# Row sums of the first batch as products with ones, fewer fillers, and conversions set back, in a fused attention and two-layer MLP kernel

## The chip, the cores and the metric

The kernel runs on one core of one Trainium2 chip. The metric is the device time of one execution in microseconds. The time before the change is 966.98 us, the median of three runs (966.38 to 970.47).

## The reference

Decayed causal attention feeds two token-wise layers. With S = 576, D = 64, four batches and eight heads:

```python
scores = q @ k.T / 8 + cum[:, None] - cum[None, :]      # cum: running sum of log f
scores = where(causal, -1e9, scores); scores -= scores.max(-1)
attn = exp(scores); attn = attn / (attn.sum(-1) + 1e-9)
x = (attn @ v) as [2304, 512]
h = max(x @ w1, x @ w2, x @ w3)            # 512 -> 768
x = h @ w_out                              # 768 -> 512
h = x @ w_in                               # 512 -> 2048
P = a0 + a1*h + a2*h**2 + a3*h**3;  Q = 1 + |b0|*|h| + |b1|*h**2
out = (P / (Q + 1e-6)) @ w_out2            # 2048 -> 512
```

The weights of the layers come as 64-bit floats, and the kernel gets their bits.

## The kernel before

**Attention.** The 32 heads go in pairs. A pair's 576 queries fall into group 0 (queries 0 to 320, in blocks 0 to 2) and group 1 (320 to 576, blocks 3 and 4). A `Unit` is one head of a pair and one group; the units in order are the slots. The first batch has eight pairs: pairs 0 to 3 do group 0 alone, two slots each, and pairs 4 to 7 group 1 alone. Later pairs do both groups, four slots. There are 64 slots, 16 of them of the first batch.

In the loop over slots (L539 to L582) three units are in flight. The newest does its `scores`: for each block, score products on TensorE into a bank with tag `s` (L343, or the split form L345 and L346), on VectorE the mask and the minimum of the negated scores in one operation (L347), on ACT the exponential, whose accumulator gives the row sums (L353). Then `normalise` adds 1e-9 to the sums and inverts them on VectorE (L358, L359), one column per block, and POOL multiplies each block by its inverse (L362). One slot later `turn` transposes the blocks on TensorE into banks with tag `t` (L382), and ACT copies them into `pt`, keys on partitions (L384). Two slots later `attend`, for the second head of the pair, does the value products of both heads into one bank with tag `o` (L398), the two heads on different columns of the array, and ACT and VectorE write the result as a high part and a low part, `x` (L405, L406).

**Fillers.** `exercised` (L80) issues `WARM` products of a constant with itself into each new bank of pairs 0 to 3 ahead of its proper use. Nothing reads them. A pair has 13 such banks: two of transposed q and k, six of scores, four of turned blocks and one of values.

**First layer.** `moe1_units` makes 18 units `moe1_h` (L423, twelve products each, a running maximum in tag `mx` with three buffers) and four units `moe1_o` (L446) per batch and group. `fill` (L504), called six times per slot, hands them out.

**Conversions.** A weight tile is loaded as raw 64-bit words by SP (L160) and turned into a high and a low single-precision part by `convert` (L162 to L179): ACT takes the magnitude, VectorE runs four operations, ACT copies the high part, POOL subtracts. `conv` has 30 of them, 18 of 128x512 for w1 to w3 and twelve of 128x256 for the first layer's output weights. Loads are traced two units ahead. The raw tiles of the 18 rotate through six buffers of tag `x2`, so that a load waits until the last VectorE operation has read the tile that held its buffer. `conv_due` sets the rate: in slots 0 to 6 each of the six calls adds 0.15 of a conversion, later 0.5.

**Order.** Each engine runs its instructions in the order of its queue. A planner that simulates the time line forms these queues: of what could run, the instruction traced earlier goes first, and `tc.high_priority` moves a block's place in that ranking. `keep_in_program_order` (`pinned`) keeps an instruction behind the one traced before it on its engine; raw loads and the copies of the decay rows (L304) on SP are pinned so. The last part of the second layer alone has an order written by hand (L766).

Of the kernel before, what the change touches and what calls it, by code (L numbers as in the profile page):

```python
# [8 lines left out]
F32 = mybir.dt.float32  # L9
# [28 lines left out]
def kernel(  # L38
# [14 lines left out]
    def r32(ap):  # L53
        return ap.bitcast(F32)
# [29 lines left out]
                nc.tensor.matmul(bank, warm[:, 0], wide, start=True, stop=True)  # L84
        return bank

    WARM = 2
    mask = const.tile([P, S], F32, name="mask")
    nc.gpsimd.memset(mask, 0.0)
    nc.gpsimd.affine_select(  # L90
# [1 line left out]
        fill=-1.0e9, base=0, channel_multiplier=1,  # L92
    )


    NR = B * H
    fl = apool.tile([NR, S], F32, name="fl", tag="vs", bufs=3)
# [15 lines left out]


    LOOK, WHOLE, PRE = 2, 6, 2
    CONV2, EARLY = (32, 0.25), 12
    kqs = {}

# [40 lines left out]
        raws[nm_] = rp.tile(shape[:-1] + [2 * shape[-1]], I32, name=f"raw_{nm_}", tag=rt, bufs=rb)  # L159
        tc.keep_in_program_order(nc.sync.dma_start(raws[nm_], src.bitcast(I32)))  # L160

    def convert(hi, lo, src, nm_, pool, tag, bufs):  # L162
        shape = list(src.shape)
        raw = raws.pop(nm_)
        raw = raw.rearrange("p c (f t) -> p c f t", t=2)
        low, top = raw[:, :, :, 0], raw[:, :, :, 1]
        t = pool.tile(shape, I32, name=f"cv_{nm_}", tag=tag, bufs=bufs)
        tf = t.bitcast(F32)
        nc.scalar.activation(tf, top.bitcast(F32), AF.Abs)
        nc.vector.tensor_scalar(tf, tf, E_LO, E_HI, op0=ALU.max, op1=ALU.min)  # L170
        nc.vector.tensor_scalar(t, t, 0x07FFFFFF, 3, op0=ALU.bitwise_and, op1=ALU.logical_shift_left)
        nc.vector.scalar_tensor_tensor(
            out=t, in0=low, scalar=29, in1=t, op0=ALU.logical_shift_right, op1=ALU.bitwise_or
        )
        nc.vector.scalar_tensor_tensor(
            out=t, in0=top, scalar=-0x40000000, in1=t, op0=ALU.bitwise_and, op1=ALU.bitwise_or
        )
        nc.scalar.activation(hi, tf, AF.Copy)
        nc.gpsimd.tensor_tensor(lo, tf, r32(hi), op=ALU.subtract)  # L179

    def rows(w):
        return w.rearrange("(c p) f -> p c f", p=P)
# [1 line left out]
    def raw_w1(fc, j):  # L184
        return rows((w1, w2, w3)[j])[:, :, fc * P : (fc + 1) * P], f"w{j}_{fc}"

    def convert_w1(fc, j):
        if fc not in w1t:
            w1t[fc] = [wpool.tile([P, 3, NDC, P], F32R, name=f"w1{x}_{fc}", tag="w", bufs=12) for x in "hl"]
        hi, lo = (t[:, j] for t in w1t[fc])  # L190
        convert(hi, lo, *raw_w1(fc, j), mpool, "x0", 6)

    def raw_wo(fc, z):
        return rows(w_out)[:, fc : fc + 1, z * 256 : (z + 1) * 256], f"wo_{fc}_{z}"
# [1 line left out]
    def convert_wo(fc, z):  # L196
        if fc not in wot:
            wot[fc] = wpool.tile([P, 2, DM], F32R, name=f"wo_{fc}", tag="x2", bufs=6)
        hi, lo = (wot[fc][:, x : x + 1, z * 256 : (z + 1) * 256] for x in range(2))
        convert(hi, lo, *raw_wo(fc, z), mpool, "x0", 6)  # L200

    wpd = dram.tile([P, NF2, 2, DM], F32R, name="wpd")

# [37 lines left out]
    class Pair:  # L241


        def __init__(self, n, b, hp, groups):
            self.n, self.b, self.hp, self.groups = n, b, hp, groups
            self.ng = groups[-1] + 1
            self.nk = GBLK[groups[-1]][-1] + 1
            self.ik = [(2 * n + h) % NKB for h in range(2)]
            self.iq = [[(2 * n + h) % m for h in range(2)] for m in NQB]
            self.pt = {}  # L250
            self.whole = n < WHOLE
            self.iqf = [(2 * n + h) % 4 for h in range(2)]

        def load(self):
# [58 lines left out]
    class Unit:  # L313
# [5 lines left out]

        def begin(self):  # L320
            self.st = apool.tile([P, 9], F32, name=f"st_{self.nm}", tag="st", bufs=3)
            self.rs = apool.tile([P, 2, 3], F32, name=f"rs_{self.nm}", tag="rs", bufs=3)

        def scores(self, i):
            p, h, g = self.pair, self.h, self.g
            if not p.whole:
                (k1, k2), (q1, q2) = k_split(p.ik[h]), q_split(g, p.iq[g][h])
            nr = P
            qs = slice(Q0[i] - GQ[g][0], Q0[i] - GQ[g][0] + P)
            keys = Q1[i]  # L330
            self.e[i] = apool.tile([P, keys], F32, name=f"e{i}_{self.nm}", tag=f"e{i}_{h}")
            e = self.e[i]
            st = self.st
            n0 = 3 * (i - GBLK[self.g][0])
            nm = st[:nr, n0 : n0 + 2]
            l = self.rs[:nr, 0, i - GBLK[self.g][0] : i - GBLK[self.g][0] + 1]
            parts = [(0, keys)] if keys <= 512 else [(0, 320), (320, keys)]
            off = S - P - Q0[i]
            for n, (a, z) in enumerate(parts):
                sp = exercised(ps_s.tile([P, 512], F32, name=f"s{i}_{n}_{self.nm}", tag="s"), p.n)  # L340
                if p.whole:
                    kf, qf = kfs[p.ik[h]][: D + 2], qfs[p.iqf[h]][: D + 2]
                    nc.tensor.matmul(sp[:nr, : z - a], qf[:, qs], kf[:, a:z], start=True, stop=True)  # L343
                else:
                    nc.tensor.matmul(sp[:nr, : z - a], q1[:, qs], k1[:, a:z], start=True, stop=False)  # L345
                    nc.tensor.matmul(sp[:nr, : z - a], q2[:, qs], k2[:, a:z], start=False, stop=True)  # L346
                nc.vector.tensor_tensor_reduce(  # L347
                    out=e[:nr, a:z], in0=sp[:nr, : z - a], in1=mask[:nr, off + a : off + z],
                    scale=-1.0, scalar=3.0e38 if n == 0 else nm[:, 0:1],
                    op0=ALU.add, op1=ALU.min, accum_out=nm[:, n : n + 1],  # L350
                )
            m = nm[:, len(parts) - 1 : len(parts)]
            nc.scalar.activation(e[:nr], e[:nr], AF.Exp, bias=m, scale=-1.0, accum_out=l)  # L353

        def normalise(self):
            blks = GBLK[self.g]
            n = len(blks)
            nc.vector.tensor_scalar_add(self.rs[:, 0, :n], self.rs[:, 0, :n], 1.0e-9)  # L358
            nc.vector.reciprocal(self.rs[:, 1, :n], self.rs[:, 0, :n])  # L359
            for j, i in enumerate(blks):  # L360
                e = self.e[i]
                nc.gpsimd.tensor_scalar(e, e, self.rs[:, 1, j : j + 1], 0.0, op0=ALU.mult, op1=ALU.add)  # L362
# [23 lines left out]
        def attend(self):  # L386
# [6 lines left out]
            ot = exercised(ps_o.tile([P, 512], F32, name=f"o_{self.nm}", tag="o"), p.n)  # L393
            order = list(GCH[g].items())
            with tc.high_priority():
                for j, (c, (col, q0)) in enumerate(order):
                    for i in (1, 0):
                        mm = nc.tensor.matmul(  # L398
                            ot[SIDES[i][0], q0 - lo : w], p.v[:, c, i], p.pt[g][:, i, col : col + hi - q0],
                            start=(j == 0), stop=(j == len(order) - 1),  # L400
                        )
                        if (j, i) != (0, 1):
                            pinned(mm)
            x = mpool.tile([P, 2, w], F32R, name=f"x_{self.nm}", tag=f"x{g}", bufs=(6, 8)[g])
            nc.scalar.activation(x[:, 0], ot[:, :w], AF.Copy)  # L405
            nc.vector.tensor_tensor(x[:, 1], ot[:, :w], r32(x[:, 0]), op=ALU.subtract)  # L406
            xt[p.b, p.hp, g] = x


    hs = {}  # L410
# [113 lines left out]
    state["c"] = state["c2"] = 0.0  # L524

    def conv_due(step):
        state["c"] += 0.15 if step < 7 else 0.5
        return NCONV - int(state["c"])

    pairs[0].load()  # L530
# [267 lines left out]
```

## Time and profile before

| what | value |
|---|---|
| median of three runs | 966.98 us |
| profiled execution | 970.9 us |
| its span, first to last instruction | 969.1 us |
| mean granted clock of TensorE | 0.988 |
| TensorE busy (PE) | 943.1 us, 97% |
| VectorE busy (DVE) | 739.6 us, 76% |
| ScalarE busy (ACT) | 623.8 us, 64% |
| GpSimd busy (POOL) | 252.4 us, 26% |

PE is TensorE's matmuls and PEld its weight loads, DVE is VectorE, ACT ScalarE, POOL GpSimd, SP the engine that issues the transfers. A line such as L362 is line 362 of the kernel below. A record of TensorE is one pass, and an fp32 matmul leaves two records, so a count of twelve in L398 is six matmuls. [...] Busy times of TensorE are modelled, since matmuls are pipelined. The shares over the whole span average stages with different limits, so the rows further down go by stage: the stretch, its length, the busy time and in brackets the instructions of each engine that took part, the granted clock, the share of the 16 DMA engines and GB/s.

### The profile page before, as it was taken

Reading aid. Unit: us, or ns where it says so; the run is one execution under the profiler, and the core shown is the slowest. Engines: PE = TensorE matmul, PEld = TensorE weight load, DVE = VectorE, ACT = ScalarE, POOL = GpSimd, SP = SyncE. Lnnn points to the kernel's source line nnn. Section 1 sums busy time; section 2 is a strip of 40 time slices with the busy share of each in tenths; the row PEclk is TensorE's granted clock in tenths of the full one; section 3 lists DMA queues with packets and bytes.
Section 4 is the critical chain, followed back from the end, with each engine's and each line's share of the span. In section 5 each row is a group of like instructions: output and inputs, shape, how many; then the busy total and the mean of one; then the engine's idle time right before and its main releaser. Section 6 shows DMA issues by size and latency. Waiting matters only on the chain.

```text
span 969.1 us, 16846 instructions
## 1 busy us (share of the span) xinstructions
PE 943.1 (97%) x5780; PEld 829.9 (86%) x5780; DVE 739.6 (76%) x1756; ACT 623.8 (64%) x1457; POOL 252.4 (26%) x408
## 2 busy tenths in 40 slices
PE   7998999999999999999999999999999999999998
PEld 6767889998998988999999978888888888999997
DVE  5789985557777777534397949988888988899997
ACT  5875666667667666646454548767666766677775
POOL 2646553445454545425133400000000000000000
PEclk9978999999999999999999999999999999999999
DMA  6685233124446445230145477011002101100000
GB/s 160 159 236 153 64 83 89 43 63 119 140 131 205 133 136 174 58 94 1 57 140 185 132 253 269 1 44 43 1 1 66 44 1 46 64 1 1 34 1 33
DMA packets 125621, 88.52 MB, mean 91 GB/s; under 512 B 74448, under 2 KB 110304, under 8 KB 125536
## 3 DMA queue, kind: packets, MB, share of 16 engines
q1 hardware_dynamic: 125536, 87.45, 30.4%
q8 instruction: 46, 0.75, 0.4%
q14 instruction: 39, 0.32, 0.1%
HBM read 64.73 MB, written 22.69 MB: 90 GB/s over the span
## 4 chain that ended last, share of the span: by engine, by line
PE 70%; DVE 14%; DMA 6%; ACT 4%; issue 3%; POOL 2%; SPq 1%; ACTq 0%; POOLq 0%; DVEq 0%
PE oo L721 7%; PE oo L722 7%; PE oo L720 7%; PE hq L671 6%; PE hq L673 6%; PE hq L672 6%; PE tp L382 4%; PE h L430 4%; PE o L398 4%; PE h L431 4%; PE h L432 4%; PE x2p L455 2%; DMA raw_wi<-in_moe_w_in_dram 2%; PE x2p L456 2%; PE x2p L457 2%
## 5 line engine op out<-in xcount | busy, mean ns | idle before, releaser
L430 PE MATMUL h<-x,w1h 128*128 128x320 f32 (+1 forms) x576 | 176.6, 307 | 3.1 <-ACT m L435 2.2
L431 PE MATMUL h<-x,w1h 128*128 128x320 f32 (+1 forms) x576 | 172.1, 299 | 0.0
L432 PE MATMUL h<-x,w1l 128*128 128x320 f32 (+1 forms) x576 | 171.2, 298 | 0.0
L430 PEld LDWEIGHTS h<-x,w1h 128*128 128x128 f32 x576 | 109.4, 190 | 7.0 <-ACT m L435 3.0
L362 POOL TENSOR_SCALAR e<-e,rs 128x64 f32<-128x64 f32 (+4 forms) x160 | 87.7, 563 | 106.4 <-DVE rs L359 91.5
L353 ACT ACTIVATE e<-e,st 128x64 f32<-128x64 f32 (+4 forms) x160 | 89.1, 557 | 37.8 <-DVE st L347 36.0
L721 PE MATMUL oo<-wp,gh 128*128 128x512 f32 x288 | 112.9, 392 | 0.0
L720 PE MATMUL oo<-wp,gh 128*128 128x512 f32 x288 | 112.5, 390 | 0.0
L431 PEld LDWEIGHTS h<-x,w1h 128*128 128x128 f32 x576 | 109.5, 190 | 0.4 <-issue 0.2
L432 PEld LDWEIGHTS h<-x,w1l 128*128 128x128 f32 x576 | 109.2, 190 | 0.0
L722 PE MATMUL oo<-wp,gl 128*128 128x512 f32 x288 | 108.8, 392 | 0.0
L680 ACT ACTIVATE s<-hq 128x512 f32<-128x512 f32 (+1 forms) x80 | 44.3, 554 | 97.4 <-PE hq L673 97.4
L347 DVE CUSTOM_DVE_ANT_0 e<-s,mask 128x320 f32<-128x320 f32 (+3 forms) x160 | 67.2, 433 | 37.9 <-PE s L346 24.0
L384 ACT ACTIVATE pt<-tp 128x384 f32<-128x384 f32 (+3 forms) x160 | 69.8, 469 | 19.2 <-PE tp L382 17.4
L683 DVE SCALAR_TENSOR_TENSOR s<-s,ab,u 128x512 f32<-128x512 f32 (+1 forms) x80 | 55.7, 697 | 32.1 <-ACT u L681 31.9
L382 PE MATMUL tp<-ident,e 128*128 128x128 f32 (+1 forms) x480 | 78.0, 280 | 1.3 <-DVE k2s L275 0.6
L673 PE MATMUL hq<-x,wil 128*128 128x512 f32 (+1 forms) x192 | 70.4, 367 | 0.0
L671 PE MATMUL hq<-x,wih 128*128 128x512 f32 (+1 forms) x192 | 70.4, 367 | 0.0
L672 PE MATMUL hq<-x,wih 128*128 128x512 f32 (+1 forms) x192 | 70.3, 366 | 0.0
L722 PEld LDWEIGHTS oo<-wp,gl 128*128 128x128 f32 x288 | 54.1, 188 | 11.7
L720 PEld LDWEIGHTS oo<-wp,gh 128*128 128x128 f32 x288 | 54.2, 188 | 11.0
L721 PEld LDWEIGHTS oo<-wp,gh 128*128 128x128 f32 x288 | 54.1, 188 | 10.9
(129 smaller groups left out, 2433.6 us busy)
## 6 DMA issues: line engine op xcount, KB each, us to landing
raw_w<-in_moe_w_dram SPq DMA_DIRECT2D x18, 512.0 KB
raw_wp<-in_moe_w_out_dram SPq DMA_DIRECT2D x32, 256.0 KB
wpd<-wp SPq DMA_DIRECT2D x32, 256.0 KB
raw_wi<-in_moe_w_in_dram SPq DMA_DIRECT2D x32, 256.0 KB
wp<-wpd SPq DMA_DIRECT2D x10, 768.0 KB
x2d<-xo SPq DMA_DIRECT2D x16, 320.0 KB
out_dram<-ob SPq DMA_DIRECT2D x18, 256.0 KB
kn<-in_k_dram SPq DMA_DIRECT2D x32, 128.0 KB
```

What stands on the lines that cost most here:

```text
L353: nc.scalar.activation(e[:nr], e[:nr], AF.Exp, bias=m, scale=-1.0, accum_out=l)
L362: nc.gpsimd.tensor_scalar(e, e, self.rs[:, 1, j : j + 1], 0.0, op0=ALU.mult, op1=ALU.add)
L382: nc.tensor.transpose(tp[:kr, dst : dst + P], self.e[i][:, Q0[c] : Q1[c]], ident)
L430: nc.tensor.matmul(hp_[:, :w], wh[:, j, dc], xs[dc][:, 1], start=(dc == NDC - 1), stop=False)
L431: nc.tensor.matmul(hp_[:, :w], wh[:, j, dc], xs[dc][:, 0], start=False, stop=False)
L432: nc.tensor.matmul(hp_[:, :w], wl[:, j, dc], xs[dc][:, 0], start=False, stop=(dc == 0))
L671: nc.tensor.matmul(hp_[:, :w], wih[:, dc, fs], xh, start=(dc == 0), stop=False)
L672: nc.tensor.matmul(hp_[:, :w], wih[:, dc, fs], xl, start=False, stop=False)
L673: nc.tensor.matmul(hp_[:, :w], wil[:, dc, fs], xh, start=False, stop=(dc == NDC - 1))
L720: nc.tensor.matmul(o, g[0][:, ts_], wh_, start=(fc == 0), stop=False)
L721: nc.tensor.matmul(o, g[0][:, ts_], wl_, start=False, stop=False)
L722: nc.tensor.matmul(o, g[1][:, ts_], wh_, start=False, stop=(fc == NF2 - 1))
```

## The change

Four edits go together. For the first batch's eight pairs (`late`) the row sums no longer come from the exponential's accumulator, and the blocks aren't normalised ahead of the transposes. In their place `attend` first issues, into a bank with tag `t`, the same products as the value products with a 128x64 tile of ones in place of the values: that gives each query's sum on 64 partitions for each head. ACT adds 1e-9 while it reads that bank, VectorE inverts the 128x320 or 128x256 result and multiplies the values by it, and the split into high and low part reads the product from SBUF. `WARM` goes from 2 to 1. `convert` gets a `behind` offset, and the 30 first conversions are traced at a priority 400 lower. The early rate goes from 0.15 to 0.3.

```diff
-    WARM = 2
+    WARM = 1
+    tiny = const.tile([P, 1], F32, name="tiny")
+    nc.vector.memset(tiny, 1.0e-9)
+    summing = const.tile([P, D], F32, name="summing")
+    nc.vector.memset(summing, 1.0)
+    LATE = 2 * NPAIR
-    def convert(hi, lo, src, nm_, pool, tag, bufs):
+    def convert(hi, lo, src, nm_, pool, tag, bufs, behind=0):
+        with tc.high_priority(offset=behind):
...
-        convert(hi, lo, *raw_w1(fc, j), mpool, "x0", 6)
+        convert(hi, lo, *raw_w1(fc, j), mpool, "x0", 6, -400)
-        convert(hi, lo, *raw_wo(fc, z), mpool, "x0", 6)
+        convert(hi, lo, *raw_wo(fc, z), mpool, "x0", 6, -400)
+            self.late = n < LATE
-            l = self.rs[:nr, 0, i - GBLK[self.g][0] : i - GBLK[self.g][0] + 1]
+            l = None if p.late else self.rs[:nr, 0, i - GBLK[self.g][0] : i - GBLK[self.g][0] + 1]
         def normalise(self):
+            if self.pair.late:
+                return
...
-                for j, (c, (col, q0)) in enumerate(order):
-                    for i in (1, 0):
-                        mm = nc.tensor.matmul(
-                            ot[SIDES[i][0], q0 - lo : w], p.v[:, c, i], p.pt[g][:, i, col : col + hi - q0],
-                            start=(j == 0), stop=(j == len(order) - 1),
-                        )
-                        if (j, i) != (0, 1):
-                            pinned(mm)
+                if p.late:
+                    sm = ps_t.tile([P, 512], F32, name=f"sm_{self.nm}", tag="t")
+                    dsts = [(sm, lambda c, i: summing), (ot, lambda c, i: p.v[:, c, i])]
+                else:
+                    dsts = [(ot, lambda c, i: p.v[:, c, i])]
+                for n, (dst, lhs) in enumerate(dsts):
+                    for j, (c, (col, q0)) in enumerate(order):
+                        for i in (1, 0):
+                            mm = nc.tensor.matmul(
+                                dst[SIDES[i][0], q0 - lo : w], lhs(c, i), p.pt[g][:, i, col : col + hi - q0],
+                                start=(j == 0), stop=(j == len(order) - 1),
+                            )
+                            if (n, j, i) != (0, 0, 1):
+                                pinned(mm)
...
-            nc.scalar.activation(x[:, 0], ot[:, :w], AF.Copy)
-            nc.vector.tensor_tensor(x[:, 1], ot[:, :w], r32(x[:, 0]), op=ALU.subtract)
+            xn = ot
+            if p.late:
+                xn = mpool.tile([P, 320], F32, name=f"xn_{self.nm}", tag="mx", bufs=3)
+                nc.scalar.activation(xn[:, :w], sm[:, :w], AF.Identity, bias=tiny)
+                nc.vector.reciprocal(xn[:, :w], xn[:, :w])
+                nc.vector.tensor_tensor(xn[:, :w], ot[:, :w], xn[:, :w], op=ALU.mult)
+            nc.scalar.activation(x[:, 0], xn[:, :w], AF.Copy)
+            nc.vector.tensor_tensor(x[:, 1], xn[:, :w], r32(x[:, 0]), op=ALU.subtract)
...
-        state["c"] += 0.15 if step < 7 else 0.5
+        state["c"] += 0.3 if step < 7 else 0.5
```

## Rows read from the trace of the kernel before

**Rows 1.** Stages: length, busy PE, PEld, DVE, ACT, POOL (count), clock, DMA, GB/s.

```profile
11.00:52.00 41.00, 40.05 (x231) 31.25 (x232) 25.02 (x91) 31.59 (x94) 19.02 (x29) 1.00 0.65 171
52.00:62.50 10.50, 9.28 (x50) 5.87 (x48) 10.38 (x29) 9.37 (x24) 2.65 (x5) 1.00 1.14 313
62.50:79.60 17.10, 15.61 (x53) 10.03 (x54) 15.81 (x35) 10.43 (x25) 11.68 (x11) 0.50 0.58 160
79.60:137.00 57.40, 52.53 (x365) 47.88 (x364) 53.73 (x126) 35.85 (x89) 33.47 (x41) 1.00 0.35 99
137.00:148.00 11.00, 8.84 (x41) 8.04 (x41) 6.67 (x19) 5.83 (x17) 6.99 (x13) 0.69 0.44 120
148.00:490.00 342.00, 338.13 (x2665) 313.18 (x2664) 208.60 (x714) 216.11 (x623) 150.77 (x271) 1.00 0.36 103
```

**Rows 2.** Chain of waits by line, 11 to 56 us, then 56 to 142.

```profile
by line: PE s L84 12.5%; DMA raw_w<-in_moe_w_dram 11.7%; PE s L343 11.0%; PE tp L84 8.7%; POOL e L362 8.3%; issue 7.3%; PE o L398 6.0%; DMA kn<-in_k_dram 5.8%; PE tp L382 4.9%; POOL w1l L179 3.4%; PE tk L297 2.9%; DVE e L347 2.3%; DVE cv_w 
...
by line: issue 8.6%; DVE cv_w L175 6.4%; DVE cv_wo L175 6.0%; DVE e L347 6.0%; PE s L343 5.6%; DVE cv_w L172 5.3%; DVE cv_wo L172 4.5%; DVE m L437 4.4%; DVE cv_wo L170 4.3%; DMA raw_w<-in_moe_w_dram 4.3%; DMA raw_wo<-in_moe_w_out_dram 4.2%;
```

**Rows 3.** Line 84 alone, two windows: busy PE, PEld (count).

```profile
4.80:11.00 6.20, 5.28 (x14) 3.03 (x14) 1.00 0.54 121
11.00:56.00 45.00, 31.18 (x90) 14.78 (x90) 1.00 0.68 185
```

**Rows 4.** Pieces of the chain from 0 to 170 us: start, us, what.

```profile
12.64 0.47 PE s L84 x2
...
36.73 1.34 PE o L398 x12
...
152.85 2.10 PE o L398 x20
```

**Rows 5.** Timeline of TensorE: start, us, instruction, idle before.

```profile
61.20 1.02 PE L343 MATMUL s<-kf,qf 66*128 66x448 f32 x2 [0.94 <-ACT qf L283]
62.53 0.90 PE L382 MATMUL tp<-ident,e 128*128 128x128 f32 x3 [0.30 <-POOL e L362]
```

**Rows 6.** ACT by form, 0 to 150 us: count, busy, mean ns, idle.

```profile
L353 ACT ACTIVATION_READ_ACCUMULATOR e<-e,st 128x1 f32 x42 | 8.0, 189 | 0.0
...
L405 ACT ACTIVATE x<-o 128x320 fp32r<-128x320 f32 x4 | 1.7, 436 | 0.9 <-PE o L398 0.9
```

**Rows 7.** VectorE by form, 148 to 490 us.

```profile
L406 DVE TENSOR_TENSOR x<-o,x 128x320 fp32r<-128x320 f32 x12 | 5.9, 491 | 2.2 <-ACT x L405 1.8
L406 DVE TENSOR_TENSOR x<-o,x 128x256 fp32r<-128x256 f32 x13 | 5.5, 420 | 16.7 <-ACT x L405 16.7
...
L359 DVE RECIPROCAL rs<-rs 128x3 f32<-128x3 f32 x24 | 4.2, 175 | 0.6
L359 DVE RECIPROCAL rs<-rs 128x2 f32<-128x2 f32 x24 | 3.9, 164 | 0.5
```

**Rows 8.** Line 359, two windows: least/median/greatest ns, starts, forms.

```profile
L359 DVE RECIPROCAL rs<-rs x8: 169/176/177, 15.2 to 51.0; 128x3 f32<-128x3 f32 x8
...
L359 DVE RECIPROCAL rs<-rs x8: 152/154/167, 61.5 to 137.3; 128x2 f32<-128x2 f32 x8
```

**Rows 9.** Tile rs by window: busy DVE, POOL.

```profile
11.00:52.00 41.00, 3.77 (x16) 11.18 (x23) 1.00 0.65 171
52.00:137.00 85.00, 4.13 (x15) 11.76 (x16) 0.90 0.49 138
```

**Rows 10.** Tile cv_w by window: busy DVE, ACT, POOL.

```profile
11.00:52.00 41.00, 13.45 (x24) 7.89 (x13) 7.97 (x6) 1.00 0.65 171
52.00:137.00 85.00, 33.26 (x48) 14.80 (x24) 17.32 (x12) 0.90 0.49 138
```

**Rows 11.** Tile cv_wo, 52 to 137 us: busy DVE, ACT, POOL.

```profile
52.00:137.00 85.00, 21.14 (x46) 8.55 (x21) 6.70 (x9) 0.90 0.49 138
```

**Rows 12.** Timeline of SP, from 65 us.

```profile
65.70 12.20 SPq L160 DMA_DIRECT2D raw_w<-in_moe_w_dram  x3
...
79.02 0.38 SPq L232 DMA_DIRECT2D v<-in_v_dram  x1
```

More of the change, by code (lines that the diff above doesn't have):

```diff
@@ L168, in convert @@
         tf = t.bitcast(F32)
[L169 to L173, printed above, removed]
-        )
[L175 to L179, printed above, removed]
+        with tc.high_priority(offset=behind):
+            nc.scalar.activation(tf, top.bitcast(F32), AF.Abs)
+            nc.vector.tensor_scalar(tf, tf, E_LO, E_HI, op0=ALU.max, op1=ALU.min)
+            nc.vector.tensor_scalar(t, t, 0x07FFFFFF, 3, op0=ALU.bitwise_and, op1=ALU.logical_shift_left)
+            nc.vector.scalar_tensor_tensor(
+                out=t, in0=low, scalar=29, in1=t, op0=ALU.logical_shift_right, op1=ALU.bitwise_or
+            )
+            nc.vector.scalar_tensor_tensor(
+                out=t, in0=top, scalar=-0x40000000, in1=t, op0=ALU.bitwise_and, op1=ALU.bitwise_or
+            )
+            nc.scalar.activation(hi, tf, AF.Copy)
+            nc.gpsimd.tensor_tensor(lo, tf, r32(hi), op=ALU.subtract)
     def rows(w):
@@ L321, in begin @@
             self.st = apool.tile([P, 9], F32, name=f"st_{self.nm}", tag="st", bufs=3)
-            self.rs = apool.tile([P, 2, 3], F32, name=f"rs_{self.nm}", tag="rs", bufs=3)
+            if not self.pair.late:
+                self.rs = apool.tile([P, 2, 3], F32, name=f"rs_{self.nm}", tag="rs", bufs=3)
         def scores(self, i):
@@ L395, in attend @@
             with tc.high_priority():
-                for j, (c, (col, q0)) in enumerate(order):
-                    for i in (1, 0):
-                        mm = nc.tensor.matmul(
-                            ot[SIDES[i][0], q0 - lo : w], p.v[:, c, i], p.pt[g][:, i, col : col + hi - q0],
-                            start=(j == 0), stop=(j == len(order) - 1),
-                        )
-                        if (j, i) != (0, 1):
-                            pinned(mm)
+                if p.late:
[9 more added lines that the diff above has]
+                                start=(j == 0), stop=(j == len(order) - 1),
+                            )
+                            if (n, j, i) != (0, 0, 1):
+                                pinned(mm)
             x = mpool.tile([P, 2, w], F32R, name=f"x_{self.nm}", tag=f"x{g}", bufs=(6, 8)[g])
-            nc.scalar.activation(x[:, 0], ot[:, :w], AF.Copy)
-            nc.vector.tensor_tensor(x[:, 1], ot[:, :w], r32(x[:, 0]), op=ALU.subtract)
             xt[p.b, p.hp, g] = x
+            xn = ot
[6 more added lines that the diff above has]
+            nc.vector.tensor_tensor(x[:, 1], xn[:, :w], r32(x[:, 0]), op=ALU.subtract)
     hs = {}
```

## The prediction

> **What bounds the kernel now.** I read the busy time by stage first. The reader is to see four regimes [rows 1]. From 148 us on TensorE is busy without pause (338.13 of 342.00 us until 490) at the full clock, and VectorE has room (208.60 of 342.00). From 11 to 52 us TensorE is busy too (40.05 of 41.00), but VectorE is not (25.02). [...] So whatever TensorE loses ahead of 148 us is not made up later, and whatever work it is spared there comes off the end. All edits fall into this part: the first batch's eight pairs and the first 30 conversions.
>
> Second, the chain of waits for the same two parts [rows 2]. From 11 to 56 us it runs through the filler matmuls of line 84 (12.5, 8.7 and 2.9 per cent in the visible shares), raw weight loads, scores and the POOL normalisation (8.3 per cent). From 56 to 142 us the conversions' VectorE lines lead it. Third, the groups of the single instructions, for prices.
>
> **Fillers (A, 11 to 56 us).** 14 and 90 of them run by 56 us [rows 3], two at each of 52 banks; 52 go. A pair takes 0.47 us of the chain [rows 4], so 0.235 us each, 12.2 us in all. The three visible shares are 24.1 per cent of 45 us, 10.8 us, and half of it goes: -5.4 us. Bounds: 0 (something else binds at once) and -12.2.
>
> **Sums with ones, first four attends.** Each repeats the value products' shape: twelve instruction records, 1.34 us [rows 4], 5.4 us in four. That is TensorE work in the stretch that TensorE sets, so I charge it by the same share as the fillers (10.8 of the 21.2 us that 90 of them cost, one half): +2.7. Bounds 0 and 5.4.
>
> **Normalisation.** In A it is 8.3 per cent of 45 us of the chain, 3.7 us. What is late next are the raw loads (11.7 per cent) and the exponentials, so half: -1.9. Bounds 0 and -3.7. In B (52 to 148 us) the recorded wait of TensorE for it in [rows 5] is 0.30 us: -0.3. On ACT 40 reads of the accumulator at 189 ns go (7.6 us) and eight evictions of a bank come (0.436 us for 320 columns, at most 3.5 us) [rows 6]; ACT is busy 31.59 of 41.00 us [rows 1], so that is cover and I count nothing.
>
> **Reciprocals and products on VectorE.** They go from a 128x3 or 128x2 tile per unit to a 128x320 or 128x256 tile per attend. No row has that size. The product is like the subtraction of line 406, 0.491 and 0.420 us [rows 7]. For the reciprocal, 175 ns for three elements and 164 for two are 11 ns an element, so 0.175 + 317 x 0.011 = 3.66 us and 0.164 + 254 x 0.011 = 2.96 us. The low end is the subtraction's row itself (0.49 and 0.42); the high end comes from the medians in the early windows, 176 and 154 ns [rows 8], 22 ns an element, 7.15 and 5.74 us. I take the middle, the row with the most instructions of this very operation, and keep both ends.
> [...]
>
> In A the four attends bring 4 x (3.66 + 0.49) = 16.6 us; VectorE has 41.00 - 25.02 = 16.0 us idle plus the 3.77 us of row-sum operations that go [rows 9]. They fit, and 3.2 us are left. In B they bring 4 x (2.96 + 0.42) = 13.5 us, with 4.13 us going [rows 9]: +9.4 us on the engine that sets the pace. Behind each such reciprocal VectorE's queue holds the next block's score reduction, for which ACT's exponential and a score bank of TensorE wait.
>
> **Conversions.** One of w1-w3 takes VectorE 13.45/6 = 2.24 us in A and 33.26/12 = 2.77 us in B [rows 10]; beside it ACT runs two instructions, POOL one, and SP a 512 KB load. Twice the early rate hands out 12 by slot 7 instead of 6, but VectorE's 3.2 us left in A hold one more: -2.8 us in B. Lower priority lets the attention's instructions pass. The twelve wo conversions cost 21.14 us before 137 us [rows 11], and only the output products of the first layer need them; behind 148 us VectorE has 133 us of room [rows 1]. Between none and all can slip; at 21.14/11.5 = 1.84 us each I take five of twelve: -9.2 (bounds 0 and -21). POOL loses 11.76 us of normalisation in 52 to 137 us [rows 9], of 47.80 us that it is busy [rows 1]; the conversions there are 0.53 us dearer than in A, 6.4 us for twelve, and if that is contention with POOL a quarter goes: -1.6 (bounds 0 and -6.4).
>
> **Sums, last four attends.** 2.10 us each at the full clock [rows 4], 8.4 us. TensorE's 9.7 us of idle time in B [rows 1] are the cover; where the pauses lie elsewhere it is not one. A quarter shows: +2.1 (bounds 0 and 8.4; at the half clock twice that). The sums also hold one of the three banks through which the transposes rotate, and the reciprocal's tile one of the three buffers of the first layer's running maximum, for 0.4 + 3.0 + 3 x 0.4 = 4.6 us by the prices above. A maximum that waits for it keeps one of the first layer's two banks, and the products behind it on TensorE stand: 0 to 4 x 4.6 us. I take 0, since two other buffers go round.
>
> **Sum.** A: -5.4 + 2.7 - 1.9 = -4.6. B: -0.3 + 9.4 - 2.8 - 9.2 - 1.6 + 2.1 = -2.4. Together -7.0 us. The profiled execution took 970.9 us (span 969.1 and 1.8 around it), so 963.9 by its own count; it lies 3.9 us above the median of 966.98, which is what the prediction is of: 960.0 us.
>
> **Rivals.** (1) The reciprocal is dear: the mechanism on the slower side. At 22 ns an element B gets 4 x (5.74 - 2.96) = 11.1 us more, on the engine that is already full there; in A 30.6 us meet 19.8, half of the excess counts (5.4), and no conversion moves (2.8). That is +19.3: 979.3 us. For it: VectorE's full rows from 52 to 137 us. Against: the larger groups say 11 ns. It decides from some 15 ns an element on, where 4 x 254 x 4 ns = 4.1 us more in B and the 2.8 have eaten the gain of 7.0.
> (2) The clock falls in A as well. Before it fell at 62.5 us TensorE had paused 0.94 us and 0.30 us [rows 5], with the fillers over since 56 us; with half the fillers such pauses can come earlier. A half-clock stretch of 17.10 us costs 8.6 us where TensorE is the bound: 968.6 us. Against: the sums' products fill part of the place.
> [...]
> (3) Only TensorE's work counts: -12.2 + 13.8 = +1.6, so 968.6 us. For it: after 148 us nothing else binds. Against: the idle and half-clock time ahead of it, which is to be had.
> (4) The loads get in the way, and the early rate does not do what it says. SP stood 12.20 us at raw loads from 65.70 us, with a v load behind it at 79.02 [rows 12]: six buffers, each free only when its conversion has read it. With 12 handed out early and the conversions behind, this comes earlier, and the copies of the decay rows are pinned behind it. Then A's 4.6 us are lost: 964.6 us.
> (5) More than I count: with the attention first in VectorE's queue TensorE no longer pauses at 60 us and keeps the full clock: -8.6 more, 951.4 us. For it: the pauses are short, 1.24 us. Against: the wide reciprocals stand in that very place.
>
> **How the numbers follow.** No change is what lies within 0.5 per cent, about what a measurement of this kernel can tell: 962.1 to 971.8 us. Forecast 0.36, with a range of its own of 955 to 966 (0.25 faster, 0.11 same); (5) 0.20, faster; (3) 0.14 and (4) 0.08, same; (2) 0.09, 0.05 same and 0.04 slower; (1) 0.13, slower. Faster 0.45, same 0.38, slower 0.17. If all pauses (10.7 us from 11 to 148 us), the half clock's 8.6 + 3.4 us and the fillers went and only the sums' 13.8 us came, it would be 946 us; the low end of 949 is just above. The high end of 976 takes in (2) twice and most of (1).
>
> **What would show it.** Right: 52 fillers; the attend of a pair twice as long; no POOL normalisation ahead of batch two; line 406's neighbour, a wide reciprocal, at 2.3 to 3.7 us; TensorE without pause from an earlier time than 148 us, by about as much as the gain; wo conversions behind that time. Wrong: a wide reciprocal of 5 us or more, or of 0.5; a granted clock of 0.5 ahead of 56 us; SP standing at raw loads ahead of 56 us with score products late behind it; VectorE full but no later than now, with the same pauses of TensorE.

## The result and the profile after

The changed kernel takes 978.28 us (median of four runs, 976.40 to 982.21) against 967.64 for the kernel before on the same chip (the 966.98 of the prediction with a fourth run). The ratio is 1.0104 with a 95% interval of 1.0085 to 1.0122: about 10 us slower, where 7 us faster was forecast. The profiled execution took 976.4 us, its span is 974.6 (before 970.9 and 969.1): it was the fastest of its four, and that of the kernel before took 3.3 us more than its median, so the two traces lie 5.5 us apart and not 10.

The stages, in the windows and columns of [rows 1]:

```profile
11.00:52.00 41.00, 37.07 (x227) 27.39 (x227) 36.99 (x93) 33.18 (x77) 10.16 (x8) 0.96 0.90 244
52.00:62.50 10.50, 8.34 (x49) 4.61 (x47) 10.50 (x21) 9.58 (x22) 4.96 (x4) 1.00 0.79 216
62.50:79.60 17.10, 13.98 (x59) 7.88 (x59) 17.00 (x35) 11.23 (x21) 5.47 (x4) 0.70 0.59 185
79.60:137.00 57.40, 48.72 (x347) 41.78 (x344) 47.99 (x115) 33.98 (x81) 22.79 (x32) 0.97 0.22 56
137.00:148.00 11.00, 10.11 (x67) 7.57 (x68) 6.34 (x26) 6.70 (x24) 5.60 (x14) 0.84 0.27 62
148.00:490.00 342.00, 340.40 (x2674) 318.19 (x2671) 203.31 (x692) 215.35 (x609) 148.07 (x266) 1.00 0.36 101
```

From 11 to 52 us VectorE has become nearly full (36.99 of 41.00 us, before 25.02), and TensorE idles 3.93 us there (before 0.95). Over the five stretches ahead of 148 us TensorE idles 18.8 us; before it was 10.7. The half clock (0.50 in the clock records, where 1.00 is full speed) does not explain that difference: in these stretches its records add up to 20.5 us, before to 23.9. From 148 us on TensorE is as full as it was.

The chain of waits by line, 11 to 56 us and 56 to 142 us, as in [rows 2]:

```profile
by line: DVE cv_w L179 15.8%; DVE xn L427 13.9%; DVE cv_w L182 11.1%; DVE e L356 10.9%; issue 10.1%; DVE cv_w L177 9.4%; DVE cv_w L178 9.2%; PE s L352 6.4%; DVE x L430 3.7%; DMA kf<-ncd 3.3%; PE s L84 3.1%; DVE xn L428 1.8%; PE tp L393 1.7%
...
by line: DVE e L356 8.6%; issue 7.3%; DVE xn L427 6.3%; DVE cv_w L182 5.9%; DVE cv_w L179 5.6%; DVE cv_wo L177 4.7%; DVE cv_w L177 4.6%; PE tp L393 4.4%; DVE cv_w L178 4.3%; DVE cv_wo L179 4.2%; DVE cv_wo L178 2.9%; DMA raw_wo<-in_moe_w_out
```

The fillers (L84) have left the head of the first chain. In their place stand four VectorE lines of conversions (cv_w, 45.5% together) and the wide reciprocal (L427, 13.9%): the chain of the first stretch, which ran through TensorE, now runs through VectorE.

Pieces of the chain from 0 to 170 us (start, us, what), beside [rows 4]:

```profile
23.59 2.14 DVE xn L427
...
109.62 1.66 DVE xn L427
127.16 2.10 PE sm L415 x20
129.26 1.95 PE o L415 x20
143.95 3.77 PE sm L415 x20
```

Two of the eight sets of products with ones (sm) stand on the chain, right ahead of the value products (o) and at the price of those at the full clock: 2.10 us, and 3.77 where the record shows the half clock (0.50 from 143.9 to 147.3 us).

VectorE by form, 0 to 160 us (count, busy, mean ns, idle before), answering to [rows 7, 8]:

```profile
L427 DVE RECIPROCAL xn<-xn 128x320 f32<-128x320 f32 x4 | 8.6, 2140 | 0.0
L427 DVE RECIPROCAL xn<-xn 128x256 f32<-128x256 f32 x4 | 7.0, 1746 | 5.2 <-ACT xn L426 5.2
...
L428 DVE TENSOR_TENSOR xn<-o,xn 128x320 f32<-128x320 f32 x4 | 1.9, 478 | 0.0
```

How much of the first layer was done ahead of 148 us is read from one of its three product lines (before L430, after L453), windows 11 to 148 and 148 to 490 us, TensorE and weight loads. The kernel before:

```profile
11.00:148.00 137.00, 23.91 (x72) 13.80 (x72) 0.91 0.53 146
```

and the changed kernel:

```profile
11.00:148.00 137.00, 17.91 (x56) 10.53 (x56) 0.93 0.52 141
148.00:490.00 342.00, 116.50 (x381) 72.14 (x381) 1.00 0.36 101
```

16 records of 0.31 us (116.50/381) are missing, and the other two lines have as many: 16 x 3 x 0.31 = 15 us of first-layer work that the kernel before had behind it at 148 us. A part was exchanged for other products, and a part comes back in smaller pauses later (TensorE idles 1.60 us from 148 to 490, before 3.87); in these two traces 5.5 us stay.

### The profile page after: what moved, and what is told of

Same layout as the page of the kernel before. It is cut to its first block, busy times and chain, and to the rows that moved or that the text cites. A ratio compares the mean times of both kernels' runs of the same rounds, so it can differ in the third digit from the quotient of the medians.

```text
span 974.6 us, 16846 instructions
## 1 busy us (share of the span) xinstructions
PE 944.1 (97%) x5856; PEld 827.6 (85%) x5856; DVE 745.4 (76%) x1742; ACT 628.1 (64%) x1425; POOL 227.3 (23%) x368
## 4 chain that ended last, share of the span: by engine, by line
PE 73%; DVE 17%; DMA 3%; issue 3%; ACT 3%; POOL 0%; SPq 0%; DVEq 0%; ACTq 0%; POOLq 0%
PE hq L696 7%; PE hq L695 7%; PE hq L694 7%; PE oo L743 7%; PE oo L745 7%; PE oo L744 7%; PE h L453 5%; PE h L455 4%; PE h L454 4%; PE tp L393 4%; PE o L415 4%; PE x2p L478 2%; PE s L354 2%; PE s L355 2%; PE x2p L480 2%
## 5 line engine op out<-in xcount | busy, mean ns | idle before, releaser
L453 PE MATMUL h<-x,w1h 128*128 128x320 f32 (+1 forms) x576 | 175.5, 305 | 4.7 <-ACT m L458 3.5
L453 PEld LDWEIGHTS h<-x,w1h 128*128 128x128 f32 x576 | 109.1, 189 | 8.3 <-ACT m L458 3.9
L373 POOL TENSOR_SCALAR e<-e,rs 128x448 f32<-128x448 f32 (+3 forms) x120 | 63.4, 544 | 90.5 <-DVE rs L370 83.0
```

Source lines behind the costliest of these rows:

```text
L453: nc.tensor.matmul(hp_[:, :w], wh[:, j, dc], xs[dc][:, 1], start=(dc == NDC - 1), stop=False)
```

## The experiments

Ratios are to the kernel before on the same chip, with their 95% interval; "us" is (ratio - 1) x 968.

| run | what | ratio (interval) | us |
|---|---|---|---|
| after | all edits | 1.0104 (1.0085 to 1.0122) | +10.1 |
| sums_only | before + sums | 1.0065 (1.0048 to 1.0082) | +6.3 |
| warm_only | before + one filler less | 1.0001 (0.9983 to 1.0019) | +0.1 |
| conv_only | before + conversions' edits | 0.9994 (0.9982 to 1.0006) | -0.6 |
| no_sums | after, no sums | 0.9967 (0.9953 to 0.9981) | -3.2 |
| sums_chunk | after, a third of the products | 1.0012 (0.9994 to 1.0030) | +1.2 |
| recip_cheap | after, copy for the reciprocal | 1.0061 (1.0037 to 1.0086) | +5.9 |
| inv_act | after, inverse on ACT | 1.0049 (1.0030 to 1.0069) | +4.7 |
| rate_back | after, early rate 0.15 | 1.0070 (1.0045 to 1.0094) | +6.8 |
| late_first | after, sums for pairs 0 to 3 | 0.9982 (0.9967 to 0.9998) | -1.7 |
| late_last | after, sums for pairs 4 to 7 | 1.0057 (1.0038 to 1.0076) | +5.5 |
| sums_cheap | sums_only with the copy | 1.0048 (1.0031 to 1.0065) | +4.6 |
| no_sums_w0 | no_sums, no filler at all | 1.0006 (0.9994 to 1.0017) | +0.6 |
| first_twice | late_first, products twice | 1.0031 (1.0015 to 1.0046) | +3.0 |
| last_twice | late_last, products twice | 1.0123 (1.0105 to 1.0141) | +11.9 |
| last_cheap | late_last with the copy | 1.0056 (1.0036 to 1.0076) | +5.4 |
| last_chunk | late_last, a fifth of the products | 1.0056 (1.0040 to 1.0071) | +5.4 |
| before_last | before + sums for pairs 4 to 7 | 1.0098 (1.0081 to 1.0115) | +9.5 |
| last_narrow | late_last, edit that cut more than was meant | 0.9908 (0.9882 to 0.9933) | -8.9 |

**Which edit.** Each of the three alone on the kernel before (fillers, sums, and the two edits of the conversions together), and the other two without the sums. The expectations name three theories. D: VectorE is crowded early on, by the conversions and the reciprocals. S: the sums are the whole cause. C: the fillers hold TensorE's clock.

```diff
# sums_only
-    WARM = 1        ->  2, rate 0.15, no -400
# no_sums
-    LATE = 2 * NPAIR
+    LATE = 0
# warm_only: LATE = 0, rate 0.15, no -400
# conv_only: LATE = 0, WARM = 2
```

> The sums with ones, the wide reciprocals and the late product alone; two fillers per bank, conversions as before. Theory D (VectorE is crowded ahead of 90 us by conversions that come twice as fast AND by the reciprocals, and the score reductions queue behind both): +2 to +6 us against before, since 15.6 us of reciprocals come where 8 us of row-sum operations go, but the conversions stay spread. Theory S (the sums are the whole cause: 12.4 us of products on TensorE and the reciprocals): +8 to +12 us, the whole loss.

> One filler per bank alone, all else as before. Theory D: -2 to -6 us, since the first stretch is bound by TensorE and the 11 us of fillers come off it, unless the clock falls earlier. Theory C (the fillers hold the clock and pace): +2 to +8 us, with a granted clock of 0.5 ahead of 56 us.

> The lower priority and the twofold early rate alone; no sums, two fillers. Theory D: +2 to +6 us: VectorE full from 20 us on, the score reductions of pairs 3 to 6 later than before by 5 us or more. Theory S: within 2 us of before, or faster, since only idle time of VectorE is filled.

> The changed kernel without the sums: one filler, lower priority, twofold rate, row sums and POOL normalisation as before. Theory D: about -2 to +3 us against before (conversions cost, fillers give). Theory S: -3 to -6 us, as the fillers give and nothing costs.

The sums alone make it slower by 6.3 us, and they turn the 3.2 us that the other edits gain into a loss of 10.1. So the sums are the edit that makes the kernel slower, and on top of the other edits they cost 13.3 us. Fillers and conversions gain nothing alone and 3.2 us together, where the prediction had credited them with 19.0. Theory S has conv_only and no_sums right; sums_only (+6.3) and warm_only (+0.1) fell between the ranges of the theories. no_sums is faster than both kernels of the change, so it is the better version.

Where the fillers' time went is seen in warm_only (11 to 52, 52 to 80 and 80 to 148 us):

```profile
11.00:52.00 41.00, 37.46 (x213) 26.84 (x213) 30.91 (x110) 35.41 (x106) 20.43 (x30) 1.00 0.76 207
52.00:80.00 28.00, 23.70 (x115) 17.29 (x116) 25.14 (x49) 17.66 (x40) 16.21 (x15) 0.76 0.75 211
80.00:148.00 68.00, 58.61 (x397) 52.04 (x396) 58.70 (x146) 41.57 (x110) 40.05 (x55) 0.97 0.32 88
```

TensorE idles 3.54, 4.30 and 9.39 us, 17.2 in all, 6.5 more than before. More than half of the fillers' 12.2 us became waiting. What became of the rest can't be read from these two traces, as they lie 2.1 us apart where the medians show no difference.

The early conversions alone show the same exchange. conv_only in windows of [rows 1]:

```profile
11.00:52.00 41.00, 36.09 (x184) 26.76 (x182) 35.33 (x87) 30.43 (x82) 22.79 (x24) 0.92 0.85 235
79.60:137.00 57.40, 53.61 (x352) 46.23 (x351) 47.89 (x126) 34.35 (x90) 30.63 (x42) 0.92 0.23 59
137.00:148.00 11.00, 11.00 (x85) 10.99 (x84) 5.62 (x17) 6.67 (x20) 5.25 (x10) 1.00 0.29 75
```

From 79.6 us on VectorE is relieved (53.51 us busy, before 60.40) and TensorE idles 3.2 us less than before. But from 11 to 52 us VectorE is busy 35.33 us in place of 25.02, and TensorE idles 4.0 us more. The value products of pair 3, the last of the first four, start 11.4 us later than before, those of pair 7 only 1.3 us later. The kernel before and conv_only, pair 3:

```profile
57.51 1.41 PE L398 MATMUL o<-pt,v 128*64 128x320 f32 x12
68.86 1.41 PE L411 MATMUL o<-pt,v 128*64 128x320 f32 x12
```

The waiting was moved ahead, and little of it was removed.

**Products or reciprocals.** In the changed kernel, one suspect at a time. Theory P: the sums cost by their products on TensorE. Theory V: they cost by the wide reciprocals on a VectorE that is full already.

```diff
# sums_chunk: sums over the first group of keys only
+                    part = order[:1] if n < len(dsts) - 1 else order
...
# recip_cheap
-                nc.vector.reciprocal(xn[:, :w], xn[:, :w])
+                nc.vector.tensor_scalar(xn[:, :w], xn[:, :w], 1.0, 0.0, op0=ALU.mult, op1=ALU.add)
# inv_act
-                nc.scalar.activation(xn[:, :w], sm[:, :w], AF.Identity, bias=tiny)
-                nc.vector.reciprocal(xn[:, :w], xn[:, :w])
+                nc.scalar.activation(xn[:, :w], sm[:, :w], AF.Ln, bias=tiny)
+                nc.scalar.activation(xn[:, :w], xn[:, :w], AF.Exp, scale=-1.0)
# rate_back
-        state["c"] += 0.3 if step < 7 else 0.5
+        state["c"] += 0.15 if step < 7 else 0.5
```

> Changed kernel, but the sum products of an attend run for its first group of keys alone (4 passes in place of 12 or 20); the other keys are left out of the sums. Everything after the sum bank (copy, wide reciprocal, product) stays. Sum products in all about 4.3 us in place of 13.8. Theory P (the sums cost TensorE's time, because it does no less work and never makes it up): about 9 us faster than the changed kernel, 968 to 971, same as before the change. Theory V (the sums cost through the wide reciprocals in a VectorE that is already full): 1 to 2 us faster at most, 976 to 978, still slower than before.

> Changed kernel with the wide reciprocal replaced by a plain VectorE copy of the same shape; the inversion is left out, every product stays. VectorE loses 15.6 us of reciprocals and gains some 3 us of copies. Theory V: most of these 12 us come off the end, since VectorE is full from 20 to 85 us: 965 to 970. Theory P: at most 2 us, 976 to 978.

> Changed kernel with the inverse made on ACT (logarithm while it reads the sum bank, then exponential of the negative) in place of ACT's addition and VectorE's reciprocal. VectorE loses 15.6 us, ACT gains eight passes of about 0.4 us (3 us). Theory V: nearly as good as the run with the cheap copy, 966 to 971, if the activation tables of the two functions need not be exchanged each time. Theory P: 976 to 978. If each use exchanges tables, slower than 978.

> Changed kernel with the early rate of conversions back at 0.15 (six handed out by slot 7 in place of twelve), the lower priority kept. Without the sums the rest of the change gained 2 us, and with them it loses 12.7 against that, where the sums alone cost 6.1; so 6.6 us come from both together. Theory V (reciprocals and early conversions meet in the same full stretch of VectorE): 4 to 6 us faster than the changed kernel, 972 to 975. Theory P: within 1 us of it.

Leaving out 9.5 us of products gains 8.9 us (0.0092 x 968): nearly one for one, as theory P has it. The changed kernel and sums_chunk begin alike, which later runs will not all do (11 to 30 us, the nine records of TensorE that are gone being mostly the first sums'):

```profile
11.00:30.00 19.00, 17.59 (x109) 13.15 (x108) 15.02 (x41) 15.85 (x37) 2.98 (x2) 1.00 0.91 253
11.00:30.00 19.00, 17.35 (x100) 12.70 (x100) 15.16 (x41) 16.49 (x39) 2.96 (x2) 1.00 0.90 254
```

The copy in place of the reciprocal spares VectorE 11.0 us and gains 4.2, the inverse on ACT 5.3: theory V holds too, for a smaller share; it had asked for 8 to 13 us and for 7 to 12. The lower early rate gains 3.3 us, below theory V's 4 to 6 and with intervals that overlap.

VectorE's rows of the copy, by form as above:

```profile
L427 DVE TENSOR_SCALAR xn<-xn 128x320 f32<-128x320 f32 x4 | 3.4, 854 | 0.0
L427 DVE TENSOR_SCALAR xn<-xn 128x256 f32<-128x256 f32 x4 | 1.2, 290 | 3.9 <-ACT xn L426 3.9
```

4.6 us in place of 15.6. And ACT's rows of inv_act:

```profile
L427 ACT ACTIVATE xn<-xn 128x320 f32<-128x320 f32 x4 | 1.9, 466 | 0.1
L427 ACT ACTIVATE xn<-xn 128x256 f32<-128x256 f32 x4 | 1.6, 411 | 0.0
L59 ACT ACT_TABLE_LOAD x1 | 1.3, 1283 | 0.7 <-PEq L806 0.7
```

One table load from 0 to 160 us, the stretch that holds all eight inversions: the logarithm and the exponential ran beside the others without a second one, so ACT's second pass of 0.41 to 0.47 us replaces 1.75 to 2.14 us on VectorE.

**First or last four attends.** The prediction priced the two halves apart (+2.7 and +2.1), so they were run apart.

```diff
# late_first
+    LATE = NPAIR
# late_last
-            self.late = n < LATE
+            self.late = NPAIR <= n < LATE
# no_sums_w0: LATE = 0 and
+    WARM = 0
```

> Changed kernel with the sums as products, the wide reciprocals and the missing normalisation for pairs 0 to 3 alone (group 0, four attends, 36 to 48 passes early); pairs 4 to 7 normalise as before. Against the changed kernel without sums (0.9967 of before, 965.6) theory P adds the products of four attends, 5.4 us: 970 to 972. Theory V, by which the reciprocals in VectorE's full stretch from 20 to 85 us decide, adds most of the whole 12.7 us, since these four are the ones that stand there: 974 to 978.

> The other half: sums as products for pairs 4 to 7 alone (group 1, four attends of 20 passes). Theory P adds their 8.4 us to 965.6: 973 to 975. My first pricing (a quarter of it shows, since TensorE pauses there anyway) would give 967 to 968. Theory V adds 1 to 3 us: 966 to 969. The two halves should make up the 12.7 us of both.

> Kernel before with the sums as products, two fillers and the old conversions, and the wide reciprocal replaced by a plain copy (the inversion is left out). With the reciprocal this cost 6.1 us over before. If the reciprocals cost only where the early conversions have filled VectorE, the copy gains 0 to 2 us here (973 to 975 on the same count) against the 4.2 us that it gained in the changed kernel. If they cost wherever they stand, it gains 4 or more: 969 to 971.

> Changed kernel without the sums and without any filler. One filler less per bank gained nothing by itself and two edits together gained 3 us. If fillers only fill pauses, taking away the last 52 gives nothing more: 964 to 967. If the clock needs them, the half-clock stretches ahead of 80 us get longer and it ends at 968 or more. If TensorE's work decides there as it does for the sums, 11 us less work gives up to 8 us: 957 to 962.

Against no_sums the first four cost 1.5 us (the intervals overlap, and both theories had asked for more), the last four 8.7, both 13.3; the halves alone make up 10.2 of it. 8.7 us is what the last four's 8.4 us of products would cost in full. Three of these four attends stand behind 80 us; the trace of no_sums, windows 11 to 80 and 80 to 148 us:

```profile
11.00:80.00 69.00, 55.33 (x254) 36.95 (x255) 63.46 (x156) 53.30 (x141) 41.78 (x44) 0.84 0.79 224
80.00:148.00 68.00, 66.38 (x458) 60.99 (x457) 50.56 (x147) 41.86 (x114) 36.12 (x55) 0.96 0.26 67
```

With the other edits TensorE is busy 66.38 of 68.00 us from 80 us on. The pauses that I had counted as the sums' cover are gone from there; they have moved ahead of 80 us (13.67 us idle from 11 to 80 us, in the kernel before 3.66).

Without any filler the kernel is 3.8 us slower than with one (no_sums_w0 against no_sums), though TensorE has 12 us less to do: on the side that the expectation gave to the clock. The mean clock from 11 to 148 us is 0.88 there and 0.90 in no_sums, that is 137 x 0.02 = 2.7 us of full-speed time. That the missing fillers lowered it is not shown. sums_cheap lies 1.6 us under sums_only, with overlapping intervals, so what the reciprocals cost where VectorE has not been filled by early conversions is not told apart from nothing.

**Do the pauses hide anything?** Products doubled in either half (on top of late_first and late_last), and the last half's parts taken away.

```diff
# first_twice, last_twice
-                    dsts = [(sm, lambda c, i: summing), (ot, lambda c, i: p.v[:, c, i])]
+                    dsts = [(sm, lambda c, i: summing)] * 2 + [(ot, lambda c, i: p.v[:, c, i])]
```

> Sums for pairs 0 to 3 alone, with their products issued twice into the same bank (the second time starts the sum anew, so the result is the same). With them once this took 966.6, 1 us over the run without sums. If TensorE's pauses ahead of 80 us (33.9 us lost there by then) hide these products, 5.4 us more of them cost 0 to 2: 966 to 969. If each product costs its time: 971 to 973.

> Sums for pairs 4 to 7 alone, with their products issued twice. Once they cost 7.7 us over the run without sums. If TensorE is full in that stretch and its products are the cost, 8.4 us more: 980 to 983. If the reciprocals or the wait behind them are the cost: 973 to 976.

> Sums for pairs 4 to 7 alone with all products, the wide reciprocal replaced by a plain copy (the inversion is left out); VectorE is spared 7.0 us less four copies of 0.3. If the products are the cost: within 2 us of the run with the last four sums, 971 to 974. If the reciprocals are: 4 to 6 us faster, 967 to 969.

> Sums for pairs 4 to 7 alone, their products for the first group of keys alone (4 of 20 passes, about 1.7 of 8.4 us; the other keys are left out of the sums). All else of the run with the last four sums stays, reciprocals included. If TensorE's products are what the last four cost: 6 to 7 us faster than that run (973.2), 966 to 968. If the wide reciprocals are: within 2 us of it.

The first four's products again, 5.4 us by [rows 4], cost 4.7 us; the last four's again, 8.4 us, cost 6.4. The expectation that pauses would hide those of first_twice failed. That run is the weaker of the two: it begins otherwise than late_first, at a mean clock of 0.91 from 11 to 30 us where late_first has 1.00. Windows 11 to 30 us of late_first and first_twice:

```profile
11.00:30.00 19.00, 17.58 (x108) 13.12 (x108) 15.21 (x41) 15.87 (x37) 3.19 (x2) 1.00 0.89 250
11.00:30.00 19.00, 17.86 (x107) 13.27 (x107) 13.48 (x36) 14.13 (x33) 3.87 (x3) 0.91 0.91 254
```

The reciprocal by itself shows no price in the last four (last_cheap, -0.1).

last_chunk goes against this: 6.7 us fewer products, no gain (-0.1). Its order of work differs from the first stretch on, before any of its sums. Windows 11 to 30 and 30 to 52 us of late_last:

```profile
11.00:30.00 19.00, 16.57 (x93) 11.95 (x93) 15.75 (x50) 16.64 (x48) 9.29 (x14) 1.00 0.92 253
30.00:52.00 22.00, 18.84 (x77) 13.20 (x76) 21.41 (x49) 15.43 (x42) 13.92 (x14) 0.69 0.79 222
```

of last_twice:

```profile
11.00:30.00 19.00, 16.64 (x94) 12.06 (x93) 15.77 (x50) 16.94 (x49) 9.27 (x14) 1.00 0.95 257
30.00:52.00 22.00, 18.24 (x76) 12.23 (x76) 22.00 (x50) 16.20 (x45) 13.92 (x14) 0.77 0.79 224
```

and of last_chunk:

```profile
11.00:30.00 19.00, 18.59 (x85) 14.34 (x83) 10.58 (x41) 13.63 (x42) 5.69 (x11) 0.73 0.86 242
30.00:52.00 22.00, 16.00 (x68) 9.84 (x67) 21.97 (x48) 15.16 (x39) 12.99 (x13) 0.84 0.74 206
```

Late_last and its doubled form begin alike (93 and 94 records, 77 and 76), so those two compare products alone. In last_chunk VectorE does 41 instructions by 30 us in place of 50, and TensorE's clock there is 0.73. What that start cost is seen at the value products of pair 3, the last ahead of any sum, in late_last, last_twice and last_chunk:

```profile
64.23 1.41 PE L415 MATMUL o<-pt,v 128*64 128x320 f32 x12
63.91 1.41 PE L415 MATMUL o<-pt,v 128*64 128x320 f32 x12
69.03 1.41 PE L416 MATMUL o<-pt,v 128*64 128x320 f32 x12
```

last_chunk is 4.8 us behind there, before the first product that it leaves out, so its time does not say that the products are free. How much of the 6.7 us they would have saved stays open. Nor is it shown why the order changed: 32 matmuls fewer stand in the ranking that the offset of 400 counts in, but sums_chunk has 48 fewer and begins as the changed kernel does.

**The cover itself.** The last four sums in the kernel before, whose idle time the prediction had counted on.

```diff
# before_last: before, with
+            self.late = NPAIR <= n < LATE
```

> Kernel before (two fillers, old conversions) with the sums as products for pairs 4 to 7 alone. This is the stretch where TensorE of the kernel before stands idle 9.7 us and where the prediction let a quarter of the 8.4 us of products show. If the idle time is a cover: at most 2 us slower than before, 968 to 970. If the products cost their time there too: 6 to 8 us slower, 974 to 976; the sums of all eight cost 6.1 us on this kernel.

It is 9.5 us slower, beyond even the expectation without cover (6 to 8): the idle 9.7 us hid nothing that shows. Up to 52 us its trace goes nearly as that of the kernel before (TensorE busy 40.41 us from 11 to 52 us, before 40.05), so the two compare the sums alone. It does not split products from reciprocals; sums_cheap puts the latter at 1.6 us for all eight, not clear of noise. It is also dearer than all eight sums on that kernel (+6.3), so there the first four, with what they drop, gained 3.2.

> As the run with the last four sums, and with as many sum products (20 passes an attend), but all except the first group of keys only 16 columns wide (the sums of the other columns lack these keys). The run that left those products out altogether gave 972.8, no gain, but its order of work differed from 11 us on: the time lost on TensorE by 52 us was 27.7 us there, 25.0 with all products, so it does not decide. With the number of instructions kept, the order should stay near. If TensorE's products are the cost of the last four: 966 to 969. If it is what the sums make wait (bank, buffer, reciprocal): 971 to 974.

last_narrow took 958.72 us, ratio 0.9908 (0.9882 to 0.9933). Its edit (`z = hi if n or j == 0 else q0 + 16`) also cut the value products of all pairs without such sums, in every batch, to 16 columns, so it leaves out much more than sums and its time says nothing of them. The case for the products rests on sums_chunk, last_twice and before_last.

## Why the prediction was wrong

**The step that failed** is the credit for the fillers and the conversions, -5.4 and -13.6 us of the sum. It rests on "whatever work it is spared there comes off the end" and on taking every relief of VectorE in B (52 to 148 us) as time of the kernel. Both edits together gave -3.2 us (no_sums), alone +0.1 and -0.6: 15.8 of the 17 us between the forecast of -7.0 and the measured +10.1. In place of a gain the runs showed waiting that came back elsewhere: TensorE idles 6.5 us more once 12.2 us of fillers are gone, and 4.0 us more ahead of 52 us once the conversions come early, against 3.2 us less from 79.6 us on.

**The sums** came out near their forecast by luck. Their terms (+2.7, +2.1, +9.4, -1.9 and -0.3) make +12.0 us; measured +13.3 on top of the other edits, and +6.3 alone. Two errors cancel in it: the products were too cheap and the reciprocals too dear.

**Products, +4.8.** The discount failed: "That is TensorE work in the stretch that TensorE sets, so I charge it by the same share as the fillers (... one half): +2.7", and "TensorE's 9.7 us of idle time in B [rows 1] are the cover ... A quarter shows: +2.1". Together 4.8 of 13.8 us. Measured, products cost 6.4/8.4 and 4.7/5.4 of their time when added, and 8.9/9.5 when taken away: 0.76 to 0.94 of it, 10 to 13 us. The idle time was no cover: before_last has it, and is 9.5 us slower. Why is argued, not shown: a filler waits for no data, while products of the sums come when the data are there and stand ahead of the values on the chain, so that a product behind a wait delays the next one rather than fills it. TensorE's recorded waits from 52 to 148 us of the kernel before are for VectorE, ACT and POOL alike, the longest:

```profile
PE h L430 <- ACT m L435: 2.2, 2, 1.2
PE x2p L456 <- POOL wo L179: 2.0, 1, 2.0
PE s L345 <- DVE q1s L287: 1.5, 1, 1.5
```

**Fillers, -5.4.** Alone +0.1 (interval -1.6 to +1.8). Half their share of the chain was too much: the lower bound of 0 that the text kept was the answer. Of the three shares that it read, the third (2.9 per cent, "PE tk L297" in [rows 2]) is a transposition of k and no filler; without it the term would have been -4.8, still too much.

**Conversions, -13.6 in three terms.** All twelve early conversions were asked for, and VectorE took more of them than the one that I allowed. Tile cv_w on VectorE, ACT and POOL, 11 to 52 and 52 to 137 us, against [rows 10]:

```profile
11.00:52.00 41.00, 24.48 (x40) 12.09 (x20) 10.16 (x8) 0.96 0.90 244
52.00:137.00 85.00, 22.52 (x32) 10.51 (x17) 14.73 (x11) 0.92 0.37 102
```

40 instructions, ten conversions, stand ahead of 52 us in place of six: 10.7 us left the later stretch, not 2.8. But of the output weights none slipped, where I had five of twelve. The tile cv_wo from 52 to 137 us, against [rows 11]:

```profile
52.00:137.00 85.00, 20.50 (x48) 9.84 (x24) 9.06 (x12) 0.92 0.37 102
```

All 48 instructions are there (46 before). Nor did they get cheaper with POOL's normalisation gone: 22.52/8 = 2.82 us each, before 2.77. So VectorE was relieved in B of about what I said by another way, and filled from 11 us on instead; by itself this was worth nothing clear of noise (-0.6), with the fillers 3.2 us.

**Reciprocals, +9.4.** Over-priced: 2.14 and 1.75 us in place of 3.66 and 2.96, 15.6 us together in place of 26.5. (2140 - 1746)/64 = 6.2 ns an element; the 11 ns taken between tiles of two and three elements did not carry over. Taking 11.0 us of them away gains 4.2, so most of their time did not show, where the text charged that of B in full. What the text feared of them (the score reduction late behind them) is on the chain: xn L427 with 13.9 and 6.3 per cent.

**Normalisation, -2.2.** Not measured by itself. In no_sums TensorE waits for it 7.4 us from 11 to 148 us in seven waits:

```profile
PE tp L389 <- POOL e L369: 7.4, 7, 3.5
```

That wait is gone in the changed kernel. As a remainder: no_sums -3.2, products 10 to 13 and reciprocals 4.2 make 11 to 14, measured 10.1; so the normalisation, ACT's reads and all interactions gave back 1 to 4 us. This is worked out, not shown.

**The sum.** Fillers and conversions 15.8 us too good (-19.0 against -3.2), the sums' products 5 to 8 too cheap, the reciprocals about 5 too dear. The first alone loses the sign: -7.0 + 15.8 = +8.8. Nor did the edits add: one by one they make +5.8, together +10.1. That they claimed the same pauses of TensorE fits this and is not shown.

**The rivals.** (1) gave the nearest time (979.3), by a mechanism that was not there: its reciprocal was to cost 22 ns an element, measured 6.2. (3), only TensorE's work, had the products in full (13.8), but credited the fillers with 12.2. The two together, products in full and fillers at nothing, were in none of the cases. (2): the half clock did come earlier, from 41.5 us for 3.4, but less of it in all (20.5 us against 23.9 from 11 to 148 us). That pauses bring it on is not shown. (4): SP's raw loads no longer stand 12.20 us; the longest group up to 90 us is 4.11, as the loads had moved forward (DMA share 0.90 in the first stretch, before 0.65):

```profile
31.51 4.11 SPq L166 DMA_DIRECT2D raw_w<-in_moe_w_dram  x3
```

Of the signs that the text named as wrong, "a granted clock of 0.5 ahead of 56 us" came true, from 41.5 us, and "VectorE full but no later than now, with the same pauses of TensorE" came near: it is full earlier, and the pauses grew.

## What to carry to other kernels

A relief of one engine is not yet a gain: 12.2 us of fillers less gave nothing here, as TensorE waited more, and conversions moved forward only moved the waiting (TensorE idle 4.0 us more from 11 to 52 us, 3.2 us less from 79.6). Nor is idle time a cover for whatever is added (before_last met 9.7 us of it and was 9.5 us slower): ask of each added instruction whether its data are there while the engine waits, and only then count on it. Give each pause to one edit alone, and price the sums of several edits by running them apart. Where a planner orders the work, an edit far on can change the order from the start (last_chunk, first_twice), so the first stretch of both traces is compared before their times are.

## What was not expected of the hardware

The wide reciprocal runs at 6.2 ns an element (128x320 in 2140 ns, 128x256 in 1746) where 128x3 against 128x2 suggested 11. A logarithm and an exponential on ACT give the same inverse in 0.50 + 0.44 us (means of inv_act's eight passes each) with one table load from 0 to 160 us, on an engine that had room (ACT busy 94.66 of 137.00 us from 11 to 148 in the changed kernel). One filler per bank is worth 3.8 us here, and the second nothing clear of noise (+0.1 us without it).
